# The first two sets of a third matrix product moved in between the last steps of the second, with another order of weight jobs, operand sums and output rows

## The chip, the cores and the metric

The kernel runs on one core of a Trainium2 chip. The metric is the time of one execution on the device, in microseconds; the median over runs is compared. The engines are TensorE (matmuls, into PSUM, which has eight banks here), VectorE, ScalarE, GpSimd and SyncE (which issues the DMAs). Each engine works through its own instructions in the order in which the program emits them, and waits where an operand or a buffer isn't free.

## The reference

A masked attention is followed by two feed-forward layers, all in float32:

```python
def _moe_ref(x, w1, w2, w3, w_out):
    h = np.maximum(np.maximum(x @ w1, x @ w2), x @ w3)
    return (h @ w_out).astype(np.float32)

def _moe2_ref(x, w_in, w_out):
    h = x @ w_in
    relu6 = np.clip(h + 3.0, 0.0, 6.0)
    g = h * relu6 / 6.0
    return (g @ w_out).astype(np.float32)

def reference(**kwargs):
    ...
    attn_out = _attn_ref(**attn_kwargs)          # (2, 8, 768, 64)
    x = np.ascontiguousarray(attn_out.transpose(0, 2, 1, 3)).reshape(B * S, H * D)
    x = _moe_ref(x=x, **moe_kwargs)              # (1536, 512), d_ff 768
    return _moe2_ref(x=x, **moe2_kwargs)         # (1536, 512), d_ff 2048
```

The weights arrive as 64-bit words; the kernel makes float32 of them itself.

## The kernel before

Only the part behind the attention matters here. It has four matrix products one after the other: the first (h, three weights and a maximum), the second (h by `w_out`, which gives X), the third (X by `w_in`, with the gate) and the fourth (the gated values by the second `w_out`). Each float32 operand is split in a high half and a low half (the rest), and each product of two tiles is three matmuls: high by high, low by high, high by low. Rows are in two batches b of 768.

**The second product** goes over (b, dh) = (0,0), (0,1), (1,1), (1,0), each with two tiles d of six steps f, six matmuls of 384 columns in a step. At the end of a tile, ScalarE empties its two banks to X (L1079); for (1,0) two ScalarE and four VectorE operations for each tile make the first operands of the third product from them at once (L1071 to L1076).

**The third product** uses Strassen's scheme in the form with seven products. A set `inset(q, b, ...)` makes one pair of column tiles for one batch; q runs from 0 to 7. Its seven products are called A11, S1, S2, A12, S3, S4 and A22 by the weight that they use, six matmuls of 384 columns each. Between them ScalarE copies A11's result into the bank on which S2 accumulates (L1155), VectorE adds partial results (e, L1163; d, L1169), and for each of four results there is a gate (ScalarE L1141, VectorE L1143) and a split (high half on ScalarE L1151, low half L1152). The operands B11, T1, T2, B21, T3, B22, T4 are sums of quarters of X, split in halves: for b = 0 by `xops` (differences L1007, high halves L1010, low halves L1012), for b = 1 by `xrest`. Both are generators, and `next(making)` takes one step of them.

**The changeover.** Before, sets (0,0) and (1,0) stand behind the end of the second product. They are interleaved with each other, the second three products behind the first.

**The main loop** has 16 stages k. A stage has a set for the products to come (none in stages 14 and 15) and the fourth product's six rows for an earlier set (`out2`), one product and one row in turn, beginning with two products. A row takes six matmuls of 512 columns into one bank, x and m in turn; then ScalarE (q = 0) or VectorE (L1201) adds it to the sums in `xF`, which share their memory with X. There is one bank x, three m and four c.

**Weight jobs.** `tick2` is one weight step: it takes each of up to three open jobs one step further, starts a load into one of two raw tiles, and opens the next job on the list `jobs`. A job `("o", q, j)` turns one raw tile into words (ScalarE L892, L894; VectorE L899, L903; one job at a time), waits for a free slot in `oslots`, makes the high half on ScalarE (L920) and the low half on GpSimd (L922). Only one o job at a time can be between its words and its low half. A job `("p", q)` takes two raw tiles, makes four sums on GpSimd (L944), waits for one of two slots in `pslots`, and makes five high halves (ScalarE L953) and five low halves (L957, on VectorE or GpSimd by WL). The slots of o(q,0) and o(q,1) are given back at the end of the stage that read them last, an odd one; there are three. So o(q,1) can be finished only when stage 2q has begun.

In a stage `tick2` is called once or twice a round, 17 times in all. Before, it is also called at every step of the second product up to (1,1), then no more until the eighth round of the changeover.

Of the kernel before, what the change touches and what calls it, by code (L numbers as in the profile page):

```python
# [57 lines left out]
XE1 = (-1, 0, -1, 0)  # L58
XS = 0
WL = (0, -2, 0, 0, 0)  # L60
WH = 2
TE = 0
TS = 8
SKA = 3
# [19 lines left out]
TN = (1, 1, 1)  # L84
OG = (-1, 1, -1, 1)
# [8 lines left out]
def body(ctx, tc, qT, kT, vP, projT, wts, consts, out):  # L94
# [745 lines left out]
    def moe(es, yp, wo):  # L840
# [31 lines left out]
        for q in range(1, 8):  # L872
            jobs += [("p", q + 1)] * (q < 7) + [("o", q, 0), ("o", q, 1)]
# [168 lines left out]

        free = list(pool_of)
        making = iter(())
        for b, dh in ((0, 0), (0, 1), (1, 1), (1, 0)):
            for d in (2 * dh, 2 * dh + 1):
                us = units(("mm", "cc")[d] if (b, dh) == (1, 0) else None)
                for f in range(6):
                    wh, wl = weight(18 + 3 * dh + f // 2, b == 1 and d % 2 and f % 2)
                    c = slice(256 * (f % 2) + 128 * (d % 2), 256 * (f % 2) + 128 * (d % 2) + 128)  # L1050
                    a, l = hT[f, b]
                    mm(us, 128, [(wh[:, c], a), (wh[:, c], l), (wl[:, c], a)], first=f == 0, last=f == 5)
                    if f % 2:
                        next(making, None)
                    if clock["job"] == NJ and not pend:
                        if (b, dh) != (1, 0) or 6 * d + f < TE:
                            tick2()
                    elif f % 2:
                        tick()
                if (b, dh) == (1, 0):  # L1060

                    if d == 0:
                        for _ in making:
                            pass
                        hi, lo = (
                            x.rearrange("p (a b) -> p a b", a=2) for x in (free.pop(0), free.pop(0))
                        )
                        x2[1, "B11"] = tuple([x[:, j, :] for j in range(2)] for x in (hi, lo))
                    u0, u1 = (u[:, 0:HF] for u in us)
                    b11, t1, t3, b22 = (blk(1, n)[:, d, :] for n in (0, 0, 1, 3))  # L1070
                    act.activation(out=hi[:, d, :], in_=u0, func=AF.Copy)  # L1071
                    act.activation(out=b11, in_=u0, func=AF.Copy)
                    dve.tensor_tensor(out=lo[:, d, :], in0=u0, in1=f32(hi[:, d, :]), op=ALU.subtract)
                    dve.tensor_tensor(out=b11, in0=u1, in1=b11, op=ALU.subtract)
                    dve.tensor_tensor(out=t3, in0=b22, in1=u1, op=ALU.subtract)
                    dve.tensor_tensor(out=blk(0, 0)[:, d, :], in0=u0, in1=t3, op=ALU.add)  # L1076
                    continue
                for hf in range(2):
                    act.activation(out=X[:, 4 * b + d, hsl(hf)], in_=us[hf][:, 0:HF], func=AF.Copy)  # L1079
            if (b, dh) == (0, 0):  # L1080
                while clock["job"] < NJ or pend:
                    tick()
                h2 = slots.pop(0)
                s4 = wo[1]
                pslots.append({
                    "A": wo[0], "B": slots.pop(0), "S2": tuple(x[:, 0:256] for x in h2),
                    "S1": tuple(x[:, 0:256] for x in s4), "S4": tuple(x[:, 256:512] for x in s4),
                })
            if (b, dh) == (0, 1):
                for _ in making:  # L1090
                    pass
                making = xops(0, [(free.pop(0), free.pop(0)) for _ in range(7)], XO[0])
                free += [x for f in range(6) for x in hT[f, 0]]
                a, b_ = ((free.pop(0), free.pop(0)) for _ in range(2))
                pslots.append({
                    "A": tuple(x[:, 0:512] for x in a), "B": tuple(x[:, 0:512] for x in b_),
                    "S1": tuple(x[:, 512:768] for x in a), "S4": tuple(x[:, 512:768] for x in b_),
                    "S2": tuple(x[:, 256:512] for x in h2),
                })
            if (b, dh) == (1, 1):  # L1100
                for _ in making:
                    pass
                tl = {n: (free.pop(0), free.pop(0)) for n in (3, 5)}
                making = xops(1, tl, (3, 5))
                oslots += [slots.pop(0), slots.pop(0), wo[2]]
        for _ in making:
            pass
        free += [x for f in range(6) for x in hT[f, 1]]
        tl = {
            n: tuple([x[:, 0:HF] for x in slots.pop(0)] for _ in range(2)) for n in (2, 6)  # L1110
        }
        making = xrest(1, tl)
        keep, free[:] = free[:4], free[4:]
        gt = [[(free.pop(0), free.pop(0)) for _ in range(2)] for _ in range(3)]
        free[:0] = keep
        acc = xF.rearrange("p a b -> p (a b)").rearrange("p (a b) -> p a b", b=512)
# [66 lines left out]

        def out2(q, b, g, tag):
            last = q == 7
            for t in range(6):
                end = last and b == 1 and t == 5
                for c0, c1 in (((0, 256), (256, 512)) if end else ((0, 512),)):
                    u = unit(tag())
                    c = slice(128 * t, 128 * t + 128)  # L1190
                    prs = []
                    for j in range(2):
                        oh, ol = weight2(("o", q, j))
                        h, l = g[j]
                        prs += [(h[:, c], oh[:, c0:c1]), (l[:, c], oh[:, c0:c1]), (h[:, c], ol[:, c0:c1])]
                    mm([u], 128, prs, c1 - c0)
# [8 lines left out]
                yield  # L1205
# [9 lines left out]
        where = {(q, 0): gt.pop(0) for q in range(2)}  # L1215
        gs = [inset(q, 0, where[q, 0], "m", t) for q, t in enumerate(("m", "x"))]
# [97 lines left out]
```

## Time and profile before

| what | value |
|---|---|
| median of 3 runs | 705.36 us (704.46 to 705.76) |
| profiled execution, its time | 704.94 us |
| profiled execution, its span (first to last instruction) | 703.2 us |
| TensorE busy | 680.7 us, 97% of the span |
| VectorE, ScalarE, GpSimd busy | 487.7, 398.4, 355.3 us |
| mean granted TensorE clock | 0.992 |

Times in the rows are microseconds from the start of the span. The second product begins at 383.5, its last quarter (1,0) at 420.97, the changeover at 433.45 and the main loop at 448.83. TensorE's matmuls overlap, so the distance between starts, not the length of one, is what a matmul costs.

### The profile page before, as it was taken

To read this page: it belongs to the slowest core of one execution; us is meant where nothing else is said; L and a number is where in the kernel's file an instruction comes from. 1 tells how busy PE (TensorE), PEld (TensorE's weight loads), DVE (VectorE), ACT (ScalarE), POOL (GpSimd) and SP (SyncE) were. 2 spreads that over 40 slices of the span, in tenths; PEclk is the share of its full clock that TensorE was granted. 3 is DMA by queue.
4 is the path that set the end of the run, shared out by engine and by line. 5 is a ranking of instruction groups with operands and counts; after the bars stand their busy time and mean duration, and the time that the engine had idled before them with its cause. 6 is when DMAs were issued, how large, how long until landed. Compare 5 with 4: busy or idle time off the path is not lost. (4 is left out here: it accounts for less than half of the span.)

```text
span 703.2 us, 13515 instructions
## 1 busy us (share of the span) xinstructions
PE 680.7 (97%) x5261; PEld 625.3 (89%) x5261; DVE 487.7 (69%) x929; ACT 398.4 (57%) x679; POOL 355.3 (51%) x281
## 2 busy tenths in 40 slices
PE   8999999999999999999999999898999999999998
PEld 7789898888889999999999999797888898888876
DVE  6888988989984444764645268854858687876654
ACT  7658789889887242432422555878545556463530
POOL 6768888999986303984733450433334324140100
PEclk9999999999999999999999999999999999999999
DMA  6665656866521001331210220021213030210004
GB/s 187 167 160 123 168 140 160 215 171 149 131 47 62 2 1 44 110 117 61 90 56 36 90 90 31 30 90 61 86 35 120 11 110 31 89 54 8 0 1 179
DMA packets 22527, 61.80 MB, mean 88 GB/s; under 512 B 3864, under 2 KB 4952, under 8 KB 22464
## 3 DMA queue, kind: packets, MB, share of 16 engines
q1 hardware_dynamic: 22032, 60.55, 29.1%
q8 instruction: 41, 0.67, 0.4%
q10 hardware_dynamic: 432, 0.40, 0.2%
q14 instruction: 22, 0.18, 0.1%
HBM read 38.87 MB, written 3.15 MB: 60 GB/s over the span
## 5 line engine op out<-in xcount | busy, mean ns | idle before, releaser
L639 POOL TENSOR_TENSOR pl<-E,ph 128x768 f16<-128x768 f32 x85 | 152.5, 1808 | 30.4 <-ACT ph L624 17.4
L571 DVE TENSOR_REDUCE mx<-m 128x1 f32<-128x384 f32 x192 | 96.7, 547 | 11.9 <-PE m L567 11.0
L621 ACT ACTIVATE E<-s 128x768 f32<-128x768 f32 x96 | 78.2, 814 | 38.7 <-PE s L617 31.3
L198 POOL TENSOR_SCALAR wr<-wraw 128x256 int32<-128x256 uint32 x36 | 45.3, 1258 | 60.7 <-DVE wy L203 57.2
L624 ACT ACTIVATE ph<-s 128x768 f16<-128x768 f32 x85 | 69.0, 811 | 0.0
L651 PEld LDWEIGHTS <-ph 128*128 128x128 f16 x576 | 54.0, 98 | 14.7 <-issue 10.4
L651 PE MATMUL x<-VV,ph 128*128 128x65 f16 x576 | 64.6, 195 | 1.3 <-DVE xo L671 0.3
L652 PE MATMUL x<-VV,ph 128*128 128x65 f16 x576 | 64.2, 196 | 0.0
L653 PE MATMUL x<-VV,pl 128*128 128x65 f16 x576 | 63.7, 193 | 0.0
L617 PE MATMUL s<-QB,KB 128*128 128x384 f32 x192 | 56.7, 376 | 0.7 <-ACT ph L624 0.7
L567 PE MATMUL m<-T,T 76*128 76x384 f32 x192 | 54.1, 353 | 3.2 <-DVE mx L571 1.5
L652 PEld LDWEIGHTS <-ph 128*128 128x128 f16 x576 | 54.5, 98 | 0.7 <-issue 0.6
L922 POOL TENSOR_TENSOR wl<-wy,wh 128x512 fp32r<-128x512 f32 x11 | 15.0, 1364 | 79.3 <-ACT wh L920 79.3
L653 PEld LDWEIGHTS <-pl 128*128 128x128 f16 x576 | 54.8, 99 | 0.0
L1201 DVE TENSOR_TENSOR xF<-x,xF 128x512 f32<-128x512 f32 (+1 forms) x43 | 29.4, 685 | 32.9 <-PE x L136 32.5
L617 PE MATMUL s<-T,T 98*128 98x384 f32 x192 | 49.6, 340 | 0.0
L216 POOL TENSOR_TENSOR wl<-wy,wh 128x512 fp32r<-128x512 f32 x24 | 36.4, 1518 | 18.0 <-ACT wh L213 17.0
L136 PE MATMUL m<-G,wh 128*128 128x384 f32 x178 | 44.5, 334 | 0.0
L1141 ACT ACTIVATE gr<-m,half 128x384 f32<-128x384 f32 x31 | 18.0, 581 | 44.9 <-PE m L1132 30.1
L567 PEld LDWEIGHTS m<-T,T 76*128 76x128 f32 x192 | 35.0, 188 | 9.2 <-DVE mx L571 5.7
L944 POOL TENSOR_TENSOR hF<-hF 128x256 f32<-128x256 f32 x8 | 6.2, 769 | 65.0 <-DVE hF L903 65.0
L136 PE MATMUL c<-G,wh 128*128 128x384 f32 x168 | 36.3, 335 | 0.9 <-DVE G L248 0.6
(337 smaller groups left out, 2057.8 us busy)
## 6 DMA issues: line engine op xcount, KB each, us to landing
wraw<-in_wts_dram SPq DMA_DIRECT2D x56, 512.0 KB
xF<-in_vP_dram SPq DMA_DIRECT2D x8, 384.0 KB
KB<-kH SPq DMA_DIRECT2D x15, 192.0 KB
QB<-qL SPq DMA_DIRECT2D x15, 192.0 KB
T<-kH SPq DMA_DIRECT2D x15, 192.0 KB
T<-qH SPq DMA_DIRECT2D x15, 192.0 KB
KB<-kL SPq DMA_DIRECT2D x15, 192.0 KB
QB<-qH SPq DMA_DIRECT2D x15, 192.0 KB
```

The costliest lines, as they stand in the source:

```text
L136: pe.matmul(u[0:m, 0:n], l, r[:, hf * n:(hf + 1) * n], start=(first and i == 0), stop=(last and i == len(pairs) - 1),)
L198: pool.tensor_scalar(out=r3[:, c], in0=raw[:, c, 0].bitcast(U32), scalar1=2.0 ** -29, scalar2=7.0, op0=ALU.mult, op1=ALU.min,)
L216: pool.tensor_tensor(out=wl, in0=f32(y), in1=f32(wh), op=ALU.subtract)
L567: pe.matmul(u[:, 0:HF], QA[h % NA][0:76, qt * 128:qt * 128 + 128], KA[h % NA][0:76, hsl(hf)], start=True, stop=True,)
L571: dve.tensor_reduce(out=mx[h][:, qt, hf:hf + 1], in_=u[:, 0:HF], axis=AX.X, op=ALU.max)
L617: pe.matmul(u[:, k, 0:HF], a[0:n, c], b[0:n, hsl(hf)], start=n == 128, stop=n < 128)
L621: act.activation(out=e, in_=u[:, :, 0:HF], func=AF.Exp, scale=BIG)
L624: act.activation(out=ph.rearrange("p (a b) -> p a b", a=2), in_=u[:, :, 0:HF], func=AF.Exp, scale=BIG,)
L639: eng.tensor_tensor(out=pl, in0=e, in1=ph, op=ALU.subtract)
L651: pe.matmul(o, ph[:, c], vv[:, 0:65], start=kt == 0, stop=False)
L652: pe.matmul(o, ph[:, c], vv[:, 65:130], start=False, stop=False)
L653: pe.matmul(o, pl[:, c], vv[:, 0:65], start=False, stop=False)
```

## The change

1. Set (0,0) and the first product of set (1,0) are emitted between the steps of the second product's quarter (1,0), from its third step on (IS, IN); the rest of set (1,0) follows alone, with one step of `xrest` behind each product. The banks of (1,0)'s two tiles change places.
2. The calls of `tick2` in the second product follow a table TQ: three more before (1,1), none in (1,1), eleven in (1,0); none in the changeover.
3. `xops` takes three steps at each f in (0,1) and (1,1), so all of them for b = 0 are called in the first half of (1,1); two at each f in (1,0).
4. In `jobs`, o(q,0) and o(q,1) come before p(q+1), not behind it.
5. For b = 0, `out2` builds its first two rows together: both halves j = 0 of the operands, then, a round later, both halves j = 1, the low half of o(q,1) last.
6. All low halves of `xrest` are made on VectorE (T2's and T4's were on GpSimd); T4's difference goes where T1 stood and is made before T2's halves; what is left of `xrest` runs on into stage 0. Of a p job, A's low half goes to VectorE and S1's to GpSimd.

```diff
-XE1 = (-1, 0, -1, 0)
+XE1 = (1, 1, 1, 1)
-WL = (0, -2, 0, 0, 0)
+WL = (1, 0, 0, 0, 0)
-TE = 0
-TS = 8
-SKA = 3
+TQ = (((1, 1, 1, 1, 3, 1), (1, 1, 1, 1, 1, 1)), ((1, 1, 1, 1, 1, 2), (1, 1, 1, 1, 1, 1)), ((0, 0, 0, 0, 0, 0), (0, 0, 0, 0, 0, 0)), ((1, 1, 1, 1, 0, 1), (1, 0, 2, 1, 1, 1)))
+TS = 0
+IS = 2
+MR = 1
+JO = 2
+IN = (1, 0, 1, 1, 1, 1, 1, 1, 0, 2)
+MK = (0, 3, 3, 2)
+LG = 1
+LE = 1
+O2 = 1
-TN = (1, 1, 1)
-OG = (-1, 1, -1, 1)
+TN = (0, 1, 1)
+OG = (1, 1, 1, 1)
...
-            jobs += [("p", q + 1)] * (q < 7) + [("o", q, 0), ("o", q, 1)]
+            x = [("o", q, 0), ("o", q, 1)]
+            x[JO:JO] = [("p", q + 1)] * (q < 7)
+            jobs += x
...
-            for n, k, i in ((1, "T1", 0), (2, "T2", 3), (4, "T3", 1), (6, "T4", 4)):
-                if n == 6:
-                    (dve if XS else pool).tensor_tensor(out=B[4], in0=B[2], in1=B[3], op=ALU.subtract)
+            for n, k, i in ((1, "T1", 0), (2, "T2", 3), (4, "T3", 1), (6, "T4", 0)):
+                if n == 2:
+                    (dve if XS else pool).tensor_tensor(out=B[0], in0=B[2], in1=B[3], op=ALU.subtract)
...
+        g0, g1 = [], []
+        sets0 = itertools.chain(inset(0, 0, g0, "m", "x"), inset(1, 0, g1, "m", "x"))
         for b, dh in ((0, 0), (0, 1), (1, 1), (1, 0)):
             for d in (2 * dh, 2 * dh + 1):
-                us = units(("mm", "cc")[d] if (b, dh) == (1, 0) else None)
+                us = units(("cc", "mm")[d] if (b, dh) == (1, 0) else None)
                 for f in range(6):
...
-                    if f % 2:
+                    for _ in range(MK[3 * b + dh - 2 * b * dh]):
                         next(making, None)
                     if clock["job"] == NJ and not pend:
-                        if (b, dh) != (1, 0) or 6 * d + f < TE:
-                            tick2()
+                        tick2(TQ[3 * b + dh - 2 * b * dh][d % 2][f])
                     elif f % 2:
                         tick()
+                    if (b, dh) == (1, 0) and 6 * d + f >= IS:
+                        for _ in range(IN[6 * d + f - IS]):
+                            next(sets0, None)
...
         def out2(q, b, g, tag):
             last = q == 7
...
+            rows = [(t, 0, 512) for t in range(6)]
+            if last and b == 1:
+                rows[5:] = [(5, 0, 256), (5, 256, 512)]
+            groups = [rows[:2]] * (b == 0 and O2) + [[x] for x in rows[2 * (b == 0 and O2):]]
+            for group in groups:
+                us = [unit(tag()) for _ in group]
+
+                def part(j, ks):
+                    for u, (t, c0, c1) in zip(us, group):
                         oh, ol = weight2(("o", q, j))
+                        h, l = (x[:, 128 * t:128 * t + 128] for x in g[j])
+                        for k in ks:
+                            pe.matmul(
+                                u[:, 0:c1 - c0], (h, l, h)[k], (oh, oh, ol)[k][:, c0:c1],
+                                start=j == k == 0, stop=j == 1 and k == 2,
+                            )
+
+                if len(group) == 1:
+                    part(0, (0, 1, 2))
+                    part(1, (0, 1, 2))
+                else:
+                    part(0, (0, 1, 2))
+                    yield
+                    part(1, (0, 1))
+                    part(1, (2,))
...
-        where = {(q, 0): gt.pop(0) for q in range(2)}
-        gs = [inset(q, 0, where[q, 0], "m", t) for q, t in enumerate(("m", "x"))]
-        for n in range(8 + SKA):
-            for j, g in enumerate(gs):
-                if n >= SKA * j:
-                    next(g, None)
-                    next(making, None)
-                    if n >= TS:
-                        tick2(TN[0])
...
+        where = {(0, 0): g0, (1, 0): g1}
+        n = 0
+        for _ in sets0:
+            next(making, None)
+            n += 1
+            if n >= TS:
+                tick2(TN[0])
+        while (1, "T2") not in x2:
+            next(making)
         for k in range(16):
...
-            for n in range(8 + LAGO):
+            lag = LE if o[1] else LG
+            for n in range(8 + lag):
+                for _ in range(MR):
+                    next(making, None)
                 next(gi, None)
                 tick2(TN[1])
-                if n >= LAGO:
+                if n >= lag:
                     next(go, None)
                     tick2(TN[2])
```

## Rows read from the trace of the kernel before

**Rows 1.** The page's first part: busy us, share of the span, instructions.

```profile
PE 680.7 (97%) x5261; PEld 625.3 (89%) x5261; DVE 487.7 (69%) x929; ACT 398.4 (57%) x679; POOL 355.3 (51%) x281
```

**Rows 2.** Busy time by stretch: length, PE, PEld, DVE, ACT, POOL, clock, DMA.

```profile
420.97:433.45 12.48, 12.48 (x74) 12.48 (x73) 10.34 (x13) 7.11 (x11) 0.00 (x0) 1.00 0.12 43
433.45:448.83 15.38, 15.10 (x86) 14.48 (x85) 13.47 (x25) 11.74 (x24) 6.16 (x5) 1.00 0.00 1
448.83:470.03 21.20, 18.02 (x79) 15.33 (x79) 15.37 (x23) 15.40 (x30) 7.17 (x7) 0.92 0.22 77
470.03:485.67 15.64, 15.64 (x79) 14.06 (x78) 5.96 (x13) 12.04 (x25) 4.17 (x4) 1.00 0.18 61
485.67:522.23 36.56, 33.13 (x157) 29.33 (x156) 26.08 (x44) 18.86 (x37) 13.07 (x14) 0.95 0.22 75
522.23:554.07 31.84, 31.57 (x157) 28.06 (x156) 23.98 (x42) 18.01 (x35) 10.40 (x10) 1.00 0.19 67
...
554.07:681.43 127.36, 126.28 (x625) 112.24 (x624) 90.21 (x156) 65.75 (x127) 30.91 (x28) 1.00 0.12 42
```

**Rows 3.** The chain that ended last, around 498 us: start, length, what.

```profile
498.06 1.39 PE x L136 x6
499.45 1.04 PE c L1132 x6
```

**Rows 4.** Timeline at the start of stage 14: start, length, instruction [idle before, releaser].

```profile
682.62 1.29 POOL L922 TENSOR_TENSOR wl<-wy,wh 128x512 fp32r<-128x512 f32 x1 [24.42 <-ACT wh L920]
...
683.97 0.50 PE L136 MATMUL x<-wl,G 128*128 128x512 f32 x1 [0.64 <-POOL wl L922]
...
684.51 0.69 DVE L1201 TENSOR_TENSOR xF<-x,xF 128x512 f32<-128x512 f32 x1 [1.72 <-PE x L136]
...
685.69 0.61 PE L136 MATMUL x<-woh,G 128*128 128x512 f32 x2
```

**Rows 5.** Timeline of all engines at the start of stage 0.

```profile
448.47 0.62 ACT L920 ACTIVATE wh<-wy 128x512 fp32r<-128x512 f32 x1
...
451.95 0.55 DVE L1152 TENSOR_TENSOR G<-g,G 128x384 fp32r<-128x384 f32 x1
...
453.60 0.63 ACT L920 ACTIVATE wh<-wy 128x512 fp32r<-128x512 f32 x1 [1.24 <-DVE wy L903]
...
454.14 0.51 ACT L1151 ACTIVATE G<-g 128x384 fp32r<-128x384 f32 x1
454.29 0.73 PE L136 MATMUL x<-wh,T 128*128 128x512 f32 x2 [2.52 <-ACT wh L920]
454.31 1.28 POOL L922 TENSOR_TENSOR wl<-wy,wh 128x512 fp32r<-128x512 f32 x1 [3.85 <-ACT wh L920]
...
454.68 1.33 DVE L1152 TENSOR_TENSOR G<-g,G 128x384 fp32r<-128x384 f32 x1 [1.11 <-ACT G L1151]
...
455.65 0.50 PE L136 MATMUL x<-wl,T 128*128 128x512 f32 x1 [0.63 <-POOL wl L922]
455.65 0.48 ACT L1155 ACTIVATE c<-m 128x384 f32<-128x384 f32 x1
```

**Rows 6.** Timeline of all engines in stage 2.

```profile
488.06 0.99 POOL L944 TENSOR_TENSOR hF<-hF 128x256 f32<-128x256 f32 x1 [10.51 <-DVE hF L903]
...
491.19 1.26 POOL L922 TENSOR_TENSOR wl<-wy,wh 128x512 fp32r<-128x512 f32 x1
...
492.50 0.50 PE L136 MATMUL x<-wl,G 128*128 128x512 f32 x1 [3.43 <-POOL wl L922]
```

**Rows 7.** Timeline of all engines at the start of stage 4.

```profile
524.56 1.29 POOL L922 TENSOR_TENSOR wol<-wy,woh 128x512 fp32r<-128x512 f32 x1 [11.46 <-ACT woh L920]
...
525.90 0.50 PE L136 MATMUL x<-wol,G 128*128 128x512 f32 x1 [0.27 <-POOL wol L922]
```

**Rows 8.** Timeline of VectorE in the second product's (1,0).

```profile
421.41 0.95 DVE L1007 TENSOR_TENSOR xF<-xF 128x768 f32<-128x768 f32 x1
...
430.49 0.96 DVE L1012 TENSOR_TENSOR G<-xF,G 128x768 fp32r<-128x768 f32 x1 [0.91 <-ACT G L1010]
```

More of the change, by code (lines that the diff above doesn't have):

```diff
@@ L1 @@
+import itertools
 from contextlib import ExitStack
@@ L1106, in moe @@
[L1106 to L1116, printed above, removed]
         def inset(q, b, g, ta, td):
@@ L1182, in inset @@
             yield
+        free = list(pool_of)
+        making = iter(())
+        g0, g1 = [], []
+        sets0 = itertools.chain(inset(0, 0, g0, "m", "x"), inset(1, 0, g1, "m", "x"))
+        for b, dh in ((0, 0), (0, 1), (1, 1), (1, 0)):
+            for d in (2 * dh, 2 * dh + 1):
+                us = units(("cc", "mm")[d] if (b, dh) == (1, 0) else None)
+                for f in range(6):
+                    wh, wl = weight(18 + 3 * dh + f // 2, b == 1 and d % 2 and f % 2)
+                    c = slice(256 * (f % 2) + 128 * (d % 2), 256 * (f % 2) + 128 * (d % 2) + 128)
+                    a, l = hT[f, b]
+                    mm(us, 128, [(wh[:, c], a), (wh[:, c], l), (wl[:, c], a)], first=f == 0, last=f == 5)
+                    for _ in range(MK[3 * b + dh - 2 * b * dh]):
+                        next(making, None)
+                    if clock["job"] == NJ and not pend:
+                        tick2(TQ[3 * b + dh - 2 * b * dh][d % 2][f])
+                    elif f % 2:
+                        tick()
+                    if (b, dh) == (1, 0) and 6 * d + f >= IS:
+                        for _ in range(IN[6 * d + f - IS]):
+                            next(sets0, None)
+                if (b, dh) == (1, 0):
+                    if d == 0:
+                        for _ in making:
+                            pass
+                        hi, lo = (
+                            x.rearrange("p (a b) -> p a b", a=2) for x in (free.pop(0), free.pop(0))
+                        )
+                        x2[1, "B11"] = tuple([x[:, j, :] for j in range(2)] for x in (hi, lo))
+                    u0, u1 = (u[:, 0:HF] for u in us)
+                    b11, t1, t3, b22 = (blk(1, n)[:, d, :] for n in (0, 0, 1, 3))
+                    act.activation(out=hi[:, d, :], in_=u0, func=AF.Copy)
+                    act.activation(out=b11, in_=u0, func=AF.Copy)
+                    dve.tensor_tensor(out=lo[:, d, :], in0=u0, in1=f32(hi[:, d, :]), op=ALU.subtract)
+                    dve.tensor_tensor(out=b11, in0=u1, in1=b11, op=ALU.subtract)
+                    dve.tensor_tensor(out=t3, in0=b22, in1=u1, op=ALU.subtract)
+                    dve.tensor_tensor(out=blk(0, 0)[:, d, :], in0=u0, in1=t3, op=ALU.add)
+                    continue
+                for hf in range(2):
+                    act.activation(out=X[:, 4 * b + d, hsl(hf)], in_=us[hf][:, 0:HF], func=AF.Copy)
+            if (b, dh) == (0, 0):
+                while clock["job"] < NJ or pend:
+                    tick()
+                h2 = slots.pop(0)
+                s4 = wo[1]
+                pslots.append({
+                    "A": wo[0], "B": slots.pop(0), "S2": tuple(x[:, 0:256] for x in h2),
+                    "S1": tuple(x[:, 0:256] for x in s4), "S4": tuple(x[:, 256:512] for x in s4),
+                })
+            if (b, dh) == (0, 1):
+                for _ in making:
+                    pass
+                making = xops(0, [(free.pop(0), free.pop(0)) for _ in range(7)], XO[0])
+                free += [x for f in range(6) for x in hT[f, 0]]
+                a, b_ = ((free.pop(0), free.pop(0)) for _ in range(2))
+                pslots.append({
+                    "A": tuple(x[:, 0:512] for x in a), "B": tuple(x[:, 0:512] for x in b_),
+                    "S1": tuple(x[:, 512:768] for x in a), "S4": tuple(x[:, 512:768] for x in b_),
+                    "S2": tuple(x[:, 256:512] for x in h2),
+                })
+            if (b, dh) == (1, 1):
+                oslots += [slots.pop(0), slots.pop(0), wo[2]]
+                for _ in making:
+                    pass
+                tl = {n: (free.pop(0), free.pop(0)) for n in (3, 5)}
+                making = xops(1, tl, (3, 5))
+                g0 += [(free.pop(2), free.pop(2)) for _ in range(2)]
@@ new lines, in moe @@
+        for _ in making:
+            pass
+        free += [x for f in range(6) for x in hT[f, 1]]
+        tl = {
+            n: tuple([x[:, 0:HF] for x in slots.pop(0)] for _ in range(2)) for n in (2, 6)
+        }
+        making = xrest(1, tl)
+        keep, free[:] = free[:4], free[4:]
+        g1 += [(free.pop(0), free.pop(0)) for _ in range(2)]
+        gt = [[(free.pop(0), free.pop(0)) for _ in range(2)]]
+        free[:0] = keep
+        acc = xF.rearrange("p a b -> p (a b)").rearrange("p (a b) -> p a b", b=512)
```

79 lines of the change are left out of this document (5 added, 74 removed).

## The prediction

> **What bounds the kernel.** I read the page's busy shares first: TensorE has work in 97% of the span [rows 1], so time can only come from its waits, and from the stretches in which they lower its clock. Then the busy time by stretch, cut where TensorE goes from one part of the program to the next [rows 2]. The last quarter (1,0) of the second product takes 12.48 us without a gap. The changeover after it, two sets of seven products, takes 15.38; stage 0 of the main loop takes 21.20, stage 1 15.64, stages 2 and 3 36.56, and every later pair of stages 31.84.
>
> What a stage needs follows from the chain of work that ended last: six matmuls of 512 columns take 1.39 us and six of 384 take 1.04 [rows 3]. A stage is seven of these products and six rows of the fourth product: 7 x 1.04 + 6 x 1.39 = 15.6, which is stage 1. Against 15.64 a stage, and 14 x 1.04 = 14.58 for the changeover, TensorE loses:
>
> - changeover: 15.38 - 14.58 = 0.80
> - stage 0: 21.20 - 15.64 = 5.56
> - stages 2 and 3: 36.56 - 31.28 = 5.28
> - five later pairs: 5 x (31.84 - 31.28) = 2.80 (one pair is shown; the four others are 127.36 / 4 = 31.84 [rows 2])
> - stage 14, which has no set: its third row starts at 685.69 [rows 4], which is 4.26 after the stage's start at 681.43, and two rows need 2.78: 1.48
>
> That is 15.9 us. The timelines say who is late. In stage 0 it is o(0,1): L920 makes o(0,0)'s high half only at 448.47, because no weight step was called between 421 and that round; o(0,1) follows through ScalarE, VectorE, ScalarE and GpSimd, and TensorE waits 2.52 and 0.63 us [rows 5]. In stage 2 it is o(1,1): on GpSimd the four sums of a p job stand ahead of L922, from 488.06 to 491.19, and TensorE waits 3.43 us [rows 6]; the stretch around it was granted 0.95 of the 2.4 GHz, so part of it ran at 1.2 [rows 2]. In stages 4, 6, ... 12 nothing stands ahead. L922 just ends at 525.85, where the sixth matmul of the first row wants it [rows 7]. Stage 14 is the same wait without products ahead of it.
>
> **The later rows (O2).** For b = 0 the first two rows are now built together: both first halves, a product in between, then both second halves. The late operand, the low half of o(q,1), was wanted after two products and five matmuls, 1.04 + 1.04 + 1.16 = 3.24 us into the stage. Now it is wanted after three products, one row's worth and four matmuls: 3.12 + 1.39 + 0.93 = 5.44. It is ready 525.85 - 522.23 = 3.62 into the stage [rows 2, 7]. So the five pairs lose nothing for 1.8 us more: **2.80 gained**. In stage 14 no product stands between: the low half comes at 683.91 [rows 4], the second halves want it 1.39 + 0.93 = 2.32 in, at 683.75. Row 2 then needs bank x back from row 0: the addition (0.69) ran 0.2 behind the last matmul [rows 4], so it frees x near 685.15. Row 2 starts there and not at 685.69: **0.54 gained**.
>
> **The order of the jobs (JO).** o(q,0) and o(q,1) now come before p(q+1). Three jobs are open at a time, and o(q,1) holds its place until its slot is free at the end of stage 2q-1; behind it wait two jobs of the next q, so p(q+2) can only open after o(q,1) is done. Counting its steps, its sums reach GpSimd in the last round of stage 2q and its halves are done in round 3 of the next one, a stage before they are wanted. So nothing stands ahead of L922 in stage 2, and with the later rows its 3.43 us and the slow clock after it go: **5.28 gained**. If a p job stayed ahead, the later rows would still cover 2.2 of the wait and 1.2 would be left; that is the lower bound.
>
> **The changeover.** TQ moves the weight steps from (1,1) (12 to none) into (1,0) (none to 11). The fifth of the eleven makes o(0,0)'s high half and the tenth o(0,1)'s low half, so stage 0's wait for them cannot come back. TensorE's own order is now: (1,0) with eight products in it (12.5 + 8.3 us, from 420.97 to 441.8), then the six left of set 1 to 448.05, where before it was 448.83. What could make it wait there?
>
> Operands of b = 0: all 18 steps are now called in the first half of (1,1). From the third difference on they took 421.41 to 431.45 [rows 8], with the chain of VectorE and ScalarE as the limit. (0,1) ends at 408.5 and its evacuations take some 0.9; B11 and T1, at the same pace, need 4.4, so the ten microseconds end at 423.8. The first product starts at 424.1 and wants the first operand only: covered. Behind these steps ScalarE still has four evacuations, two splits, p1's five conversions and two word conversions, some 6.3 us at 0.3 to 0.85 each, from 422.8 on, before it copies product A11 for S2, at 429.1 (an estimate); TensorE comes to S2 at 429.3. I take nothing, with 1 us as the other end.
>
> Set 1 alone: the six products come 1.04 us apart, with nothing of the second product between them. S3 must wait for the sum e, which stands on VectorE behind the four operations that empty (1,0)'s last banks: 0.5.
>
> Then the queues fall behind. T2's and T4's low halves move from GpSimd to VectorE (XE1). At 441.8 the eighth product ends; ScalarE copies it and then makes the first evacuation, so VectorE starts at 442.9. It has 15 operations of 128x384 up to the last gate of set 1, and T1's low half, 0.95. The 15 take 0.55 each, or 0.47 where they overlap: 8.0 to 9.2 us. GpSimd's difference B21 - T2 now falls in among them, and a low half that meets GpSimd took 1.33 where it took 0.55 alone [rows 5]: 0.8 more. The last gate is done between 450.9 and 452.9. ScalarE, in order behind it, has a high half, T4's two and then the copy for stage 0's S2, four operations of 0.48 to 0.51 [rows 5], 2.0 us: the copy is done at 452.9 to 454.9. TensorE wants it after two products and one row's worth, 448.55 + 3.47 = 452.0. So the wait is 0.9 to 2.9; I take 2.0.
>
> Does the clock fall? After waits of 2.52 + 0.63 stage 0 lost another 2.4 at a granted clock of 0.92; after 3.43 another 1.9 at 0.95 [rows 2]; in stage 14, with a wait of about 1, another 0.5. For 2.0 I take 1.0, between 0 and 2.4. The changeover and stage 0 then lose 0.5 + 2.0 + 1.0 = 3.5 in place of 6.36: **2.86 gained**. The ends are a gain of 6.36 and a loss of 0.4 (1 + 0.5 + 2.9 + 2.4 = 6.8).
>
> The rest costs nothing: A's low half on VectorE and S1's on GpSimd (WL) lie a stage ahead of their use, and the number of matmuls, loads and bytes is the same.
>
> **Sum.** 2.80 + 0.54 + 5.28 + 2.86 = 11.5 off the profiled execution's 704.94: 693.4. The median of the runs stands 0.4 above it: **693.9**. With the best end of each term it is 689.4; with the worst (-0.4 + 4.1 + 2.8 + 0) 698.9.
>
> **Rivals.**
>
> *The changeover costs nothing* (chance 0.17): VectorE's operations overlap better than I count and the copy comes in time. For it: 0.9 of the wait rests on small overlaps. Then 693.9 - 3.5 = 690.4.
>
> *The order of the jobs does not help* (0.08): the p jobs come later now, and p2, which wants two raw tiles, two resources and five conversions, is not done for stage 2, or GpSimd meets L922 after all. Against it: p2 counts as done in round 3 of stage 1. Then the 5.28 comes back: 699.2.
>
> *Bank x is short* (0.12). Row 0 keeps x until its second half, and row 2 wants it one product later, where before a row and two products lay between. The addition ends 0.7 after the pair, the product gives 1.04: 0.35 of margin. An operation of 0.69 ahead of the addition on VectorE costs 0.35, two cost 1.0. In seven stages that is 2.5 to 7: about 699.
>
> *Slower* (0.05): the same wait for x, with the clock falling each time. If each of the seven stages waits 0.7 and loses 2.0 to the clock, that is 18.9, and the time is 712. It decides from 11.5 / 7 = 1.6 a stage. Against it: waits of 0.27 in each later pair left the granted clock at 1.00 [rows 2, 7]. A page of the Trainium skill speaks for it: TensorE: Matmul & The Clock Gate, section "A second HAM failure mode: psum-queue depth-cycling", tells of a kernel in which short idle times between groups, as it went round its PSUM banks, made the clock fall and rise again and again. By that rule the time would be 712; the rows at hand do not agree with it so far.
>
> My forecast has 0.55, and 0.03 is left for what I don't see. About 0.2% is what a measurement of this kernel can tell from no change. The cases give faster 0.91, same 0.03, slower 0.06. The range takes in the free changeover and most of a short bank x: 690.3 to 698.7.
>
> **What would show it.** Right: no wait for L922 in stages 0 to 13 and pairs of stages of 31.3; no wait of TensorE in (1,0); one wait of c in stage 0, for the copy on ScalarE (L1155's successor). Wrong: waits of x for the addition of row 0, a wait of stage 2's first product for p2, or waits of c inside (1,0). A granted clock below 1 in any later stage would be the slow rival's mark.

## The result

The changed kernel takes 693.42 us (median; 692.21 to 695.09) beside 705.15 for the kernel before on the same chip: a ratio of 0.9836, with a 95% interval of 0.9813 to 0.9858. Forecast were 693.9 and a range of 690.3 to 698.7. A second measurement of the same kernel (e11) gave 693.41 and 0.983 [0.9805, 0.9854].

The profiled execution took 695.09 us, the longest of those timed, with a span of 693.3. The page's first part, busy time by engine; it answers to [rows 1]:

```profile
PE 677.0 (98%) x5261; PEld 625.8 (90%) x5261; DVE 484.4 (70%) x933; ACT 400.7 (58%) x679; POOL 343.6 (50%) x277
```

Busy time by stretch, columns as in [rows 2]: the quarter (1,0) with the eight products in it, the six products left of set 1, stage 0, stage 1, stages 2 and 3, 4 and 5, six more, and stages 12 and 13.

```profile
421.04:441.87 20.83, 20.83 (x121) 20.82 (x121) 16.36 (x25) 16.06 (x32) 7.53 (x6) 1.00 0.15 51
441.87:449.10 7.23, 6.42 (x37) 6.10 (x37) 5.97 (x11) 4.88 (x10) 1.85 (x1) 1.00 0.00 1
449.10:468.71 19.61, 17.56 (x80) 15.32 (x79) 12.75 (x24) 14.89 (x30) 1.34 (x1) 0.91 0.23 80
468.71:484.35 15.64, 15.64 (x79) 14.06 (x79) 8.20 (x15) 10.75 (x22) 6.85 (x8) 1.00 0.10 36
484.35:515.63 31.28, 31.28 (x157) 28.12 (x157) 23.26 (x40) 19.01 (x37) 9.30 (x10) 1.00 0.19 68
515.63:546.91 31.28, 31.28 (x157) 28.11 (x157) 23.86 (x41) 18.41 (x36) 9.27 (x10) 1.00 0.19 68
546.91:640.75 93.84, 93.84 (x469) 84.34 (x469) 71.51 (x123) 55.27 (x106) 27.82 (x30) 1.00 0.19 68
640.75:672.00 31.25, 31.25 (x157) 28.08 (x157) 20.81 (x36) 13.99 (x27) 2.60 (x2) 1.00 0.00 1
```

From stage 1 to stage 13 TensorE is busy without a gap: each pair of stages takes 31.28 or 31.25. The waits behind 300 us are three, by TensorE's list of waits (line waited for, us in total, times, longest):

```profile
PE c L1067 <- ACT c L1090: 2.0, 1, 2.0
PE c L1067 <- DVE c L1098: 0.8, 1, 0.8
PE x L1214 <- DVE xF L1232: 0.5, 1, 0.5
```

They stand in stage 0 (the copy of A11's product for S2), in set 1 (the sum e for S3) and in stage 14 (bank x). The timeline of stage 0 shows why the copy is late:

```profile
446.68 1.85 POOL L1030 TENSOR_TENSOR xF<-xF 128x768 f32<-128x768 f32 x1 [6.87 <-DVE T L1047]
...
447.66 1.29 DVE L1087 TENSOR_TENSOR G<-g,G 128x384 fp32r<-128x384 f32 x1
...
452.35 0.55 DVE L1078 SCALAR_TENSOR_TENSOR g<-gr,c 128x384 f32<-128x384 f32 x1
...
452.93 0.52 ACT L1086 ACTIVATE G<-g 128x384 fp32r<-128x384 f32 x1
453.36 0.51 ACT L1035 ACTIVATE wh<-xF 128x384 fp32r<-128x384 f32 x1
453.77 0.51 ACT L1035 ACTIVATE wl<-xF 128x384 fp32r<-128x384 f32 x1
454.18 0.47 ACT L1090 ACTIVATE c<-m 128x384 f32<-128x384 f32 x1
...
454.71 0.62 PE L1067 MATMUL c<-wh,wh 128*128 128x384 f32 x2 [2.05 <-ACT c L1090]
...
456.63 1.05 PE L1214 MATMUL m<-wh,G 128*128 128x512 f32 x2
```

VectorE ends set 1's last gate at 452.90. ScalarE has stood behind it, and makes a high half and T4's two before the copy. TensorE gets it at 454.65. The low half at 447.66 takes 1.29 us while GpSimd's difference runs beside it, and 0.55 elsewhere. After the wait a pair of matmuls of 512 columns takes 1.05 where 0.62 is the rule: from 456 to 458 the granted clock is 0.50, which is 1.2 GHz, and over all of stage 0 it is 0.91.

In stage 2, GpSimd has nothing ahead of o(1,1)'s low half, and the matmul that reads it comes 1.8 us after its end, 487.82; this answers to [rows 6]:

```profile
486.52 1.30 POOL L932 TENSOR_TENSOR wl<-wy,wh 128x512 fp32r<-128x512 f32 x1 [8.63 <-ACT wh L930]
...
489.62 0.39 PE L1214 MATMUL x<-wl,G 128*128 128x512 f32 x1
```

Stage 14 begins at 671.86; its third row, which wants x, comes 3.84 later, where two rows need 2.78 [rows 4]:

```profile
673.06 1.31 POOL L932 TENSOR_TENSOR wl<-wy,wh 128x512 fp32r<-128x512 f32 x1 [24.55 <-ACT wh L930]
...
674.96 0.69 DVE L1232 TENSOR_TENSOR xF<-x,xF 128x512 f32<-128x512 f32 x1 [1.73 <-PE x L1214]
...
675.70 0.72 PE L1214 MATMUL x<-woh,G 128*128 128x512 f32 x2 [0.55 <-DVE xF L1232]
```

By the prediction's own measure, the length of a stretch less what its matmuls need, TensorE now loses 7.23 - 6.25 = 0.98 in set 1, 19.61 - 15.64 = 3.97 in stage 0, nothing in stages 1 to 13, and 3.84 - 2.78 = 1.06 in stage 14: 6.0 in place of 15.9. The difference, 9.9, is that of the spans, 703.2 - 693.3.

### The profile page after: what moved, and what is told of

Its sections match the earlier page's. It is cut to its first block, busy times and chain, and to the rows that moved or that the text cites. A ratio compares the mean times of both kernels' runs of the same rounds, so it can differ in the third digit from the quotient of the medians.

```text
span 693.3 us, 13524 instructions
## 1 busy us (share of the span) xinstructions
PE 677.0 (98%) x5261; PEld 625.8 (90%) x5261; DVE 484.4 (70%) x933; ACT 400.7 (58%) x679; POOL 343.6 (50%) x277
## 4 chain that ended last, share of the span: by engine, by line
PE 69%; DVE 3%; ACT 1%; issue 0%; POOLq 0%; DVEq 0%
PE c L144 13%; PE x L1214 10%; PE m L144 10%; PE c L1067 9%; PE m L1214 9%; PE m L1067 7%; PE m L273 4%; PE x L144 3%; PE s L625 2%; PE x L659 1%; PE x L660 1%; PE x L661 1%; DVE mx L579 1%; PE m L687 0%; PE m L575 0%
## 5 line engine op out<-in xcount | busy, mean ns | idle before, releaser
L1086 ACT ACTIVATE G<-g 128x384 fp32r<-128x384 f32 x64 | 33.5, 523 | 29.0 <-DVE g L1078 28.6
L1087 DVE TENSOR_TENSOR G<-g,G 128x384 fp32r<-128x384 f32 x64 | 37.4, 584 | 6.9 <-ACT G L1086 6.9
L1214 PE MATMUL x<-wh,G 128*128 128x512 f32 (+1 forms) x134 | 41.8, 393 | 0.0
```

Source lines behind the costliest of these rows:

```text
L1214: pe.matmul(u[:, 0:c1 - c0], (h, l, h)[k], (oh, oh, ol)[k][:, c0:c1], start=j == k == 0, stop=j == 1 and k == 2,)
```

## The experiments

Each time is a median, each ratio is to the kernel before on the same chip.

**e1: the rows one by one, all else as changed.**

```diff
-O2 = 1
+O2 = 0
```

> The changed kernel with the later rows undone (O2 = 0), all else kept. Theory (the low half of o(q,1) is the late operand at every even stage, and the rows built together give it 2.2 us): the low half is wanted 3.24 us into the stage again and comes at 3.6, so each of stages 2, 4, ... 12 loses 0.56 and stage 14 loses 0.4 more: pairs of stages of 31.8 in place of 31.28, the time 3.8 us over the changed kernel, about 697. Rival (the order of the jobs alone brings the half in time, the rows built together do nothing): pairs of 31.28 and the time of the changed kernel, 693.4.

697.04 us, 0.9887 [0.9847, 0.9927]. The timeline of stage 2, and a later pair of stages by stretch:

```profile
484.21 1.29 POOL L932 TENSOR_TENSOR wl<-wy,wh 128x512 fp32r<-128x512 f32 x1 [8.63 <-ACT wh L930]
...
485.56 0.50 PE L1214 MATMUL x<-wl,G 128*128 128x512 f32 x1 [0.27 <-POOL wl L932]
...
498.24:530.08 31.84, 31.57 (x158) 28.06 (x157) 23.75 (x42) 18.43 (x35) 9.26 (x10) 1.00 0.19 66
```

The same wait stands in each even stage from 2 to 12, and a pair takes 31.84 again, at a granted clock of 1.00. So without the paired rows the 0.56 a pair come back, whatever else the change does.

**e2: the p job first, all else as changed.**

```diff
-JO = 2
+JO = 0
```

> The changed kernel with the old order of the jobs (p(q+1) before o(q,0), JO = 0), all else kept. Theory J (the order is what took the four sums of a p job away from in front of L922): stages 2 and 3 take 32.5 or more again, since the rows built together cover only 2.2 of the 3.4 us; time 694.6 to 698.7. Theory T (the weight steps called in (1,0) did it, because every job is now further on when stage 2 begins; by a count of steps p3's sums come in round 7 of stage 1): stages 2 and 3 take 31.28, time 693.4.

697.79 us, 0.9877 [0.9851, 0.9903]. Stage 2 by the timeline of all engines:

```profile
486.55 0.98 POOL L954 TENSOR_TENSOR hF<-hF 128x256 f32<-128x256 f32 x1 [10.24 <-DVE hF L913]
...
489.70 1.71 POOL L932 TENSOR_TENSOR wl<-wy,wh 128x512 fp32r<-128x512 f32 x1
...
491.46 0.50 PE L1214 MATMUL x<-wl,G 128*128 128x512 f32 x1 [1.71 <-POOL wl L932]
```

The sums stand ahead of the low half again, and paired rows cover only a part of it. That the weight steps come earlier (TQ) does not do it; the order of the jobs does. Here the rival of the short bank also appears: in stages 4 to 10 TensorE's weight load waits 0.3 for x, four times in all, because an operation of a weight job stands ahead of row 0's addition on VectorE. In stage 4:

```profile
524.11 0.68 DVE L1232 TENSOR_TENSOR xF<-x,xF 128x512 f32<-128x512 f32 x1
...
524.84 0.30 PEld L1214 LDWEIGHTS x<-wh,G 128*128 128x128 f32 x2 [0.30 <-DVE xF L1232]
```

That pair takes 31.54, at a granted clock of 1.00.

**e3 and e4: the kernel before, with paired rows alone, and with the order of the jobs as well.** e3 adds the changed `out2` and `O2 = 1` to the kernel before. e4 also has:

```diff
-            jobs += [("p", q + 1)] * (q < 7) + [("o", q, 0), ("o", q, 1)]
+            jobs += [("o", q, 0), ("o", q, 1)] + [("p", q + 1)] * (q < 7)
```

> The kernel before with the paired rows alone. Theory: the five later pairs of stages fall from 31.84 to 31.28 (2.8 us) and stage 14 gains 0.4; in stage 2 the p job's sums still stand ahead of L922, 2.2 of the 3.43 us are covered, and the clock does not fall for what is left: 4.1 gained. In stage 0 nothing is gained: S2 needs ScalarE's copy of A11, which stands behind o(0,1)'s conversion and two word conversions until 456.1, so the wait only moves from the row to the product. Sum 7.3, about 697.8. Rival (stage 0's wait is for o(0,1) alone, which the paired rows would cover but for 1.3 us): another 4 us less, about 693.6.

> As the run before it, and the order of the jobs of the changed kernel (o(q,0), o(q,1), then p(q+1)), with the old steps and the old changeover. Theory J: no sums ahead of L922 in stage 2, stages 2 and 3 take 31.28, another 1.2 us less than with the paired rows alone, about 696.6. Theory T (only the earlier steps bring this): stages 2 and 3 as with the paired rows alone, 697.8. Stage 0 loses its 5.5 in either case.

e3: 700.52 us, 0.9925 [0.9897, 0.9954]; some 2.7 more than expected. Stage 0 gains nothing, as forecast: its wait moves to S2, 3.71. Stage 2 still waits for the sums' sake, 1.71 where 1.2 was expected, and a later pair takes 31.68, not 31.28, since the weight load waits 0.43 for x, as in e2. e4: 696.51, 0.9865 [0.9841, 0.9889], as expected. Its waits in stages 2 to 12 are gone, and a pair takes 31.28. The pair of e3, and that of e4:

```profile
506.45:538.13 31.68, 31.57 (x157) 28.09 (x157) 23.59 (x42) 17.95 (x35) 10.43 (x10) 1.00 0.20 67
...
487.33:518.61 31.28, 31.28 (x157) 28.12 (x157) 23.21 (x40) 19.12 (x37) 9.56 (x10) 1.00 0.19 68
```

Stage 0 of e4 has no wait for o(0,1); it waits at S2, for the copy, longer than the changed kernel does:

```profile
457.66 0.62 PE L1133 MATMUL c<-wh,wh 128*128 128x384 f32 x2 [3.44 <-ACT c L1156]
```

So two edits, the paired rows and the order of the jobs, bring 1 - 0.9865 = 1.35% of the 1.64% by the medians. The moved set, its weight steps and the operand steps are left for the rest, some 2 us (0.3% of 705). The times don't show it, since the intervals overlap. The traces point the same way: from the start of the changeover to the end of stage 0 e4 takes 35.97 us where 14.58 + 15.64 are needed and loses 5.75, at a granted clock of 0.92 in stage 0; the changed kernel loses 4.95 at 0.91, and 3.23 in e11 at 1.00. At like clock that is 0.8, so what these edits bring by themselves stays open, and they were not tried one by one. And the two edits want each other: with the p job first the paired rows run short of bank x (e2, e3), and alone they gain 0.16 a pair and not 0.56; with the o jobs first they don't run short.

**e5: the operand steps later.** Steps of `xrest` come behind the products and not ahead of them, five in the changeover, and T4's difference behind T2's halves. One of its three places in the program:

```diff
-                for _ in range(MR):
-                    next(making, None)
                 next(gi, None)
+                next(making, None)
                 tick2(TN[1])
```

> The changed kernel, but T3's and T4's steps are called behind stage 0's products and not ahead of them, and GpSimd's difference for T4 behind T2's halves. Theory (ScalarE's queue in order, and behind it VectorE's, make the copy of A11 late for stage 0's S2): the copy no longer stands behind T3's and T4's high halves, 1.2 us, and no low half of set 1 meets the GpSimd operation, 0.7: the wait of 2.05 falls to 0.2 to 0.6 and the clock stays up, so stage 0 takes 16.0 to 16.5 in place of 19.6, the time about 690. Rival (the copy waits for the gates alone, which these steps don't hold up): the wait stays at 1.5 or more, stage 0 at 18.5 or more, 692.5 to 693.4.

692.91 us, 0.9834 [0.9801, 0.9866]. The wait for the copy falls from 2.05 to 1.19, and S3 keeps its 0.80, but the first row's own evacuation is now late (0.32):

```profile
452.82 0.62 PE L1067 MATMUL c<-wh,wh 128*128 128x384 f32 x2 [1.19 <-ACT c L1090]
...
456.90 0.73 PE L1214 MATMUL x<-wh,G 128*128 128x512 f32 x2 [0.32 <-ACT xF L1230]
```

The copy's wait lost 0.86 of the 1.45 to 1.85 that were expected, stage 0 takes 17.73 where 16.0 to 16.5 were, and the time is the rival's. It does not tell e5 from the changed kernel.

**e6: two of `xrest`'s low halves back on GpSimd.**

```diff
-XE1 = (1, 1, 1, 1)
+XE1 = (1, 0, 1, 0)
```

> The changed kernel with T2's and T4's low halves on GpSimd again. Theory (VectorE's load in the changeover sets the copy): two operations of 0.47 less ahead of the last gate, so the wait of 2.05 falls to about 1.1, stage 0 to 18 or less, the time about 692. Rival (what GpSimd does in that stretch holds VectorE up by as much, 1.33 in place of 0.55 for a low half): the wait stays at 2 or grows, 693.4 or more.

694.65 us, 0.9858 [0.9824, 0.9893]. The theory fell, and the rival was right: the wait for the copy grows to 2.50 (the trace shows it; the interval takes in the changed kernel's ratio). VectorE has less to do, but what it does takes longer beside GpSimd: two of set 1's low halves take 1.28 and 1.30 here, one took 1.29 in the changed kernel. The second:

```profile
449.34 1.02 POOL L1038 TENSOR_TENSOR wh<-xF,wh 128x384 fp32r<-128x384 f32 x1 [0.37 <-ACT wh L1035]
...
450.44 1.30 DVE L1087 TENSOR_TENSOR G<-g,G 128x384 fp32r<-128x384 f32 x1 [0.59 <-ACT G L1086]
...
455.63 0.62 PE L1067 MATMUL c<-wh,wh 128*128 128x384 f32 x2 [2.50 <-ACT c L1090]
```

**e7: a third bank for the rows of stages 14 and 15**, where no set uses the c banks:

```diff
             tags["n"] += 1
+            if tags["n"] > 84:
+                return ("c", "x", "m")[tags["n"] % 3]
```

> The changed kernel, with rows in stages 14 and 15 on three kinds of banks (x, m, c in turn) and not two. Theory (row 2 of stage 14 waits for the addition that empties x): its wait of 0.55 goes, the third row starts 3.3 us into the stage in place of 3.84, nothing else changes: 0.5 us less, hardly to be seen in the time. Rival (the wait is for the low half of o(7,1), which the row before needs): the third row starts at 3.8 as before.

693.51 us, 0.9853 [0.9807, 0.9899]. Stage 14 begins at 671.20, its third row at 674.33 with no wait in between: 3.13 in place of 3.84, so 0.7 of the 1.06 was the bank. The median can't tell 0.7 from nothing.

```profile
674.33 0.62 PE L1214 MATMUL c<-woh,G 128*128 128x512 f32 x2
```

**e8: e5 and e7, and more of VectorE's work put off.** The last two operations of (1,0)'s evacuation come behind set 1's second product of the changeover, and set 1's last split into stage 0. The first of these, in part:

```diff
+                    def rest(t3=t3, b22=b22, u0=u0, u1=u1, d=d):
+                        dve.tensor_tensor(out=t3, in0=b22, in1=u1, op=ALU.subtract)
+                        dve.tensor_tensor(out=blk(0, 0)[:, d, :], in0=u0, in1=t3, op=ALU.add)
```

> The operand steps behind, the third kind of bank at the end, and two more of the same kind: the last two operations that empty the second product's last banks stand behind the sum e of set 1, and set 1's last split behind stage 0's first product. Theory: the wait of 0.81 before S3 goes, the copy is in time, stage 0 takes 15.7 to 16, stage 14 gains 0.5: 0.8 + 3.7 + 0.5 = 5.0 less than the changed kernel, about 688.5. Rival (VectorE has no room, what is put behind comes back as another wait of set 1 or stage 0): 690 or more.

693.12 us, 0.9845 [0.9807, 0.9883]. The rival was right: the waits come to 2.72, beside 0.81 + 2.05 = 2.86 in the changed kernel, only elsewhere. They are now 1.03 at S4, 0.40 at S2 and 1.29 at the first row:

```profile
448.26 1.32 PE L1067 MATMUL c<-G,T 128*128 128x384 f32 x6 [1.03 <-DVE x L1104]
...
453.45 0.62 PE L1067 MATMUL c<-wh,wh 128*128 128x384 f32 x2 [0.40 <-ACT c L1090]
...
458.50 0.73 PE L1220 MATMUL x<-wh,G 128*128 128x512 f32 x2 [1.29 <-ACT xF L1236]
```

**e9, e10 and e11 on one chip: work taken out of the stretch, e5 with e7, and the changed kernel again.** e9 puts three of set 1's four splits, and T1's low half, behind the products that waited; it has the order of steps of e5, the third bank of e7 and the late evacuation of e8 too. In part:

```diff
-            def split():
-                if later:
+            def split(go=not hold):
+                if later and go:
...
+                next(making, None)
+                if k == 0 and n < 3:
+                    aside[0]()
```

> Theory (VectorE and ScalarE have more to do between the last products of (1,0) and stage 0's S2 than the stretch has time for, so a wait goes only when work leaves the stretch): three of set 1's four splits (1.0 us each on ScalarE and VectorE) now lie behind stage 0's S2, and T1's low half and the rest of (1,0)'s last evacuation behind S3's sum. The waits of S3, of stage 0's S2 and of its first row, 2.86 us together in the changed kernel, come to at most 1.2; with the third bank at the end, 0.7 off stage 14, the time is about 691. Rival (the waits are kept and only change place, as when the same work was only shuffled): 2.5 to 3 us again, now at the products of stage 0 that want T1, T2 or the gates, and about 693.

> The two single edits that gained a little, put together: the operand steps behind the products and their sets, and a third bank for the rows of the last two stages. If they are independent, waits of about 2.3 us in place of 2.86 before the first row and 0.35 in place of 1.06 lost in stage 14: 1.2 to 1.3 us less than the changed kernel, about 692. If the time lies within 0.5 of the changed kernel's on the same chip, what is gained in the waits is below what the runs tell apart.

> The changed kernel itself, for the comparison on the same chip and for the clock. Theory (the clock falls after a 2.05 us wait in some executions and not in others): the same waits, 0.81, 2.05 and 0.72, and stage 0's stretch at a granted clock of either 0.91 with 3.9 to 4.0 us lost or 1.00 with 2.3 lost; about 693. Rival (the fall belongs to the kernel): 0.91 again, and the difference from the run with the third bank would be that kernel's own.

e9: 692.75, 0.9823 [0.9797, 0.9849]. e10: 692.62, 0.982 [0.9792, 0.9849]. e11: 693.41, 0.983 [0.9805, 0.9854]. In e9 the waits of S3 and S2 are gone, as expected. But 1.81 and 0.69 come in their place, 2.5 together, and the time is 692.75: the rival's numbers (2.5 to 3, about 693), not the theory's (at most 1.2, about 691). The 1.81 is for the evacuation of the first row, which stands on ScalarE behind a weight job, T3's high half and a split:

```profile
452.49 0.64 ACT L930 ACTIVATE woh<-wy 128x512 fp32r<-128x512 f32 x1 [2.71 <-DVE wy L913]
...
453.03 0.65 ACT L902 ACTIVATE wy<-wraw 128x512 f32<-128x512 f32 x1
...
453.58 0.65 ACT L904 ACTIVATE wr<-wraw 128x512 int32<-128x512 uint32 x1
...
454.13 0.83 ACT L1045 ACTIVATE T<-xF 128x768 fp32r<-128x768 f32 x1
454.87 0.51 ACT L1088 ACTIVATE G<-g 128x384 fp32r<-128x384 f32 x1
455.28 0.58 ACT L1240 ACTIVATE xF<-x 128x512 f32<-128x512 f32 x1
...
455.91 0.73 PE L1224 MATMUL x<-wh,G 128*128 128x512 f32 x2 [1.81 <-ACT xF L1240]
```

Then a weight load waits 0.69 for T3's low half. What the three kernels and the first profile lose, from the changeover's six products (6.25 without waits) to the end of stage 0 (15.64):

| kernel | six products | stage 0 | lost | waits named | clock in stage 0 |
|---|---|---|---|---|---|
| changed, first profile | 7.23 | 19.61 | 4.95 | 0.81 + 2.05 | 0.91 |
| changed, again (e11) | 7.16 | 17.96 | 3.23 | 0.80 + 2.04 | 1.00 |
| e10 | 7.16 | 17.72 | 2.99 | 0.80 + 1.22 + 0.32 | 1.00 |
| e9 | 6.29 | 19.64 | 4.04 | 1.81 + 0.69 | 0.91 |

The two stage 0 rows of e11 and e9, by stretch:

```profile
448.96:466.92 17.96, 15.92 (x80) 13.99 (x79) 12.69 (x24) 14.75 (x30) 1.34 (x1) 1.00 0.25 83
```

```profile
446.99:466.63 19.64, 17.76 (x80) 14.97 (x79) 14.89 (x25) 14.94 (x31) 3.13 (x2) 0.91 0.24 81
```

The first two rows of the table are one program with the same waits to 0.01 us. They differ by 1.65 in stage 0 and in the granted clock: what the clock took is a matter of the execution. The other runs bear this out. e1, e2 and e7 have the same wait for the copy, 2.02 to 2.03, and e6 one of 2.50, and all were granted 1.00 in stage 0; e9 was granted 0.91 after one of 1.81. So with waits of 1.8 to 2.5 us the length alone does not say whether the clock falls. After the waits of 3.71 (e3), of 3.44 (e4) and of 2.52 and 0.63 (before) stage 0 was granted 0.92 each time. Of the 3.23 that e11 loses 0.39 stands in none of the waits named and not in the clock: a wait costs somewhat more than its length, as in e1, where 0.27 cost a pair 0.56.

The waits of e10 come to 2.34, as expected. Neither e9 nor e10 is shown to beat the changed kernel: the intervals overlap, and the medians lie within 0.8.

**e12: e9, with the weight steps of stage 0's first rounds made up for later, and T3's halves and the splits behind the first rows.** T4's difference comes behind the first row's evacuation too; that evacuation writes its sum over a quarter of X which the difference reads, so T4's values are not the reference's here. The instructions and their sizes are the same.

```diff
-                tick2(TN[1])
+                early, more = k == 0 and n < 3, k == 0 and 3 < n
+                tick2(0 if early else TN[1] + more)
...
-                next(making, None)
-                if k == 0 and n < 3:
+                for _ in range((0, 0, 2)[n] if early else 1):
+                    next(making, None)
+                if k == 0 and 2 <= n < 5:
                     aside[0]()
```

> In the last of the reordered kernels the rows' evacuation on ScalarE stood behind three operations of weight steps (0.64 + 0.65 + 0.65), a high half of T3 (0.83) and a split (0.51), and TensorE waited 1.81 us for it, then 0.7 for T3's low half, at a granted clock of 0.91; from set 1's last six products to stage 1 it lost 4.0 us. Here the weight steps, T3 and the splits of stage 0 come behind that evacuation (the weight steps are made up for in the stage's later rounds). Theory (each wait is an order on one engine, so the right order leaves none): no wait for the evacuation, at most 0.7 for T3's low half, clock 1.00, 0.3 to 1.0 us lost in the two stretches and about 690. Rival (the work in the stretch is too much in any order): another wait of 1.5 to 2.5 us, now at stage 0's S3 or in stage 1 or 2 where the weight steps come late, and about 692.5.

696.46 us, 0.9887 [0.9855, 0.9919]: slower than e9 by more than 3. The evacuation is in time, and T3's and T4's low halves are late instead, by 2.85 and 2.03:

```profile
459.11 0.44 PE L1069 MATMUL c<-T,wh 128*128 128x384 f32 x1 [2.85 <-DVE T L1047]
...
467.85 0.44 PE L1069 MATMUL c<-wh,wh 128*128 128x384 f32 x1 [2.03 <-DVE wh L1035]
```

The theory that the right order leaves no wait is not borne out by this order; the waits, 4.88 together, even exceed the 1.5 to 2.5 of the rival. That the work is too much in any order isn't shown by one order.

## Why the prediction was right

Term by term, against what it gave:

- **The later rows in five pairs, 2.80 gained.** Right in size and cause: each pair takes 31.28, and with the rows one by one (e1) each takes 31.84. The prediction gave this to the paired rows alone; they need the order of the jobs beside them (e3: 31.68).
- **The order of the jobs, 5.28.** Right: stages 2 and 3 take 31.28. The count of when o(1,1) is done was borne out (nothing ahead on GpSimd, a margin of 1.8). e2 gave the other bound too: with a p job ahead the paired rows leave a wait of 1.71, where 1.2 was worked out. The sums stand 2.4 into the stage, as before; but the low half itself took 1.71 beside VectorE's work, not 1.26.
- **Stage 14, 0.54.** 0.42: the addition frees x at 675.65, 3.79 into the stage, where 3.72 was counted.
- **The changeover, 2.86 (3.5 lost in place of 6.36).** The places were right: S3 waits 0.81 (0.5 was forecast) for e on VectorE, and the copy comes 2.05 late (2.0), with the gate at 452.9 (450.9 to 452.9) and the copy at 454.65 (452.9 to 454.9). That the 2.0 was met is in part luck: the copy is near the late end of its range, and TensorE wants it at 452.66, not at 452.0. No wait came in (1,0): ScalarE copies A11's product at 428.49, 0.6 earlier than estimated. The clock's 1.0 was neither of the two values that occur: 1.65 between two executions with equal waits, or nothing. 4.95 is lost in the first profile and 3.23 in the second. The sum with the second, 2.80 + 5.28 + 0.42 + (6.36 - 3.23) = 11.6, is the difference of the medians, 11.7. Of the 3.13 in it that the changeover gained, 6.36 - 4.95 = 1.41 stand between two profiles in both of which the clock fell; the rest is there only where it kept its level. The sum came out because errors cancelled: 1.0 was charged for a clock that kept its level (as it did in three of the four executions timed, 0.998 in the mean, beside 0.993 in the profiled one), against 0.3 too little for S3, 0.1 for stage 14 and the 0.4 that is lost beside the named waits. The prediction had taken all that is lost beside a wait for the clock's.
- **Nothing for the rest.** Right: no wait stands in stages 1 to 13.

**The rivals.** A free changeover: no, 3.2 to 5.0 are lost. The order of jobs of no help: no (e2). Bank x short: not in the changed kernel, but the margin is as thin as was said; with a weight operation ahead of the addition (e2, e3) it costs 0.3 to 0.4 a pair. The slow one, with the clock falling at each wait for x, did not come: those waits of 0.3, and e1's 0.27 in each even stage, left the granted clock at 1.00. The Trainium skill, TensorE: Matmul & The Clock Gate, section "A second HAM failure mode: psum-queue depth-cycling", tells of a clock that rises and falls when TensorE idles briefly between groups often enough; once in 31.5 to 31.8 us, as here, these waits did not make it fall, and no run here has them more often. After a single wait of some 2 us the runs show both outcomes.

**What stays open.** Whether the last 3 us between the changeover and stage 1 can be had. In e5, e8, e9 and e12 every order that took a wait from one product gave one to another that needs ScalarE or VectorE, and e6 took none. That the order is to blame and not the amount of work isn't settled: both engines are busy 12.7 to 14.9 of some 18 us in stage 0, so the amount alone doesn't fill them. Why the clock falls in one execution and not in another is open too.

## What to carry to other kernels

Subtract, stage by stage, what the matmuls need from what the stage takes, and name for each rest the one instruction that comes late: here the rests gave the median within a microsecond, though the term of the changeover came out by errors that cancelled. A stall that recurs in each round is mended by asking for the late operand one product later, and a single one by the order in which a helper engine gets its jobs; these two edits together brought most of the gain, four fifths by the medians, and neither does it alone. Where a stretch has one wait and two helpers in a chain, moving work about hands the wait to the next product: look first at who stands behind the moved instruction in its queue.

## What the runs showed of the hardware that was not expected

- One program, equal waits of 0.8 and 2.05 us: in one execution the stretch behind them was granted 0.91, in another 1.00, with 1.65 us between them. Waits of 2.02 to 2.50 in e1, e2, e6 and e7 left it at 1.00, one of 1.81 in e9 came with 0.91.
- A low half of 128x384 on VectorE takes 0.55 us alone, and 1.28 to 1.33 in the rows of set 1 and [rows 5] where a subtraction on GpSimd runs beside it. In the changed kernel GpSimd's difference ends at 448.53 and the low half that meets it at 448.95; in e9 a low half took 2.02 us (448.24 to 450.26) beside the same difference (448.00 to 449.84):

```profile
448.00 1.84 POOL L1041 TENSOR_TENSOR xF<-xF 128x768 f32<-128x768 f32 x1 [9.19 <-DVE T L1047]
...
448.24 2.02 DVE L1035 TENSOR_TENSOR wh<-xF,wh 128x384 fp32r<-128x384 f32 x1
```

  Both end 0.42 behind GpSimd's operation, which is less than the 0.55 that one takes alone; so does the 1.33 of [rows 5], and the two of e6 end 0.42 and 0.41 behind. So nearly the whole of it waits for GpSimd to end. The Trainium skill, SBUF — State Buffer, section "Who interferes with whom", says that the two engines share a pair of ports under an exclusive lock, and that a VectorE instruction with two SBUF inputs contends with a GpSimd instruction that reads SBUF; the rows agree. Work given to GpSimd to relieve VectorE thus made VectorE later (e6). GpSimd's low half of 128x512 in its turn took 1.71 in e2, beside VectorE's work, and 1.29 to 1.31 in the rows of e1 and of the changed kernel.
